# Chunked linear recurrence and squared-ReLU feed-forward: K, B, V and A turned by transposing DMAs, first feed-forwards one batch at a time

## The chip, the cores and the metric

The kernel runs on one core of a Trainium2 chip. The metric is the device time of one execution in microseconds (us); lower is better. The engines are called by the profile's names: PE is TensorE (PEld its weight loads), DVE VectorE, ACT ScalarE, POOL GpSimd and SP SyncE, which here only issues DMAs.

## The reference

Six inputs r, k, v, w, a, b have the shape (4, 8, 768, 40): batch, heads, time, head dimension. A state of 40 x 40 for each of 32 heads runs over time, and its output goes through a feed-forward with 2048 hidden units.

```python
for t in range(S):
    y[:, :, t] = np.einsum('bhd,bhde->bhe', rt, state)
    Sa = np.einsum('bhde,bhe->bhd', state, at)
    state_decay = state * wt[:, :, None, :] - np.einsum('bhd,bhe->bhde', Sa, bt)
    state = state_decay + np.einsum('bhd,bhe->bhde', vt, kt)
x = y.transpose(0, 2, 1, 3).reshape(B * S, H * D)      # 3072 x 320
g = np.maximum(x @ w_in, 0.0) ** 2                     # 3072 x 2048
out = g @ w_out                                        # 3072 x 320
```

Inputs and outputs are float32; the kernel multiplies in bfloat16, save for the cumulative sum of the logarithms of w, which is float32.

## The kernel before, in words

**Tiling.** Time is cut into six chunks of 128. The code calls a *batch* m one chunk of one batch element: m runs from 0 to 23, four to a chunk. A batch holds 128 positions (partitions) by 8 heads by 40. A *step* st is two of the four head pairs of a batch, so there are 48 steps. A pair of heads is padded to 2 x 64 = 128 columns, so that one 128 x 128 transpose on PE turns one pair.

**Preparation of a batch** (`add_prep`). SP loads six tiles of 160 KB (W, K, B, A, V, R; line 244), each in a ring of four buffers ("N"), so loads can run four batches ahead. ACT takes the logarithm of W (L257), PE the cumulative sum (cs, L263), ACT its exponentials GI and GA (L268). POOL multiplies K and B by GI into KB (L279; for the first two batches DVE takes B) and casts A into GA, and V and R into RV (L290), and V into EVX (L285). PE turns three sets, eight transposes each, all at line 294: tGA (GA and A), tKB (K and B) and tRV (R and V), each into one PSUM bank. The banks are emptied by ACT (GT, L330; KBT, L342) and DVE (AT = turned A times GT, L336; RVT, L347). KB has a ring of five buffers, GA and RV of two each, KBT of three.

**A step of the scan** (`add_step`). PE multiplies KBT by AT (ca, L394), DVE masks the product (CN, L402), PE forms P (L411, L417) and corrects it twice (L426) with ACT's Mc (L529) and DVE's c1 (L439) between them, ACT writes Sn (L536), POOL keeps two check values (x1, L443; Cc, L447). A later part turns back Sn (L463, L469; DVE TB, L474), multiplies by the turned R and V (ex, L482), masks (DVE EVX, L487), multiplies by KB (kbm, L498) and by the turned R (z, L505). DVE then writes the step's output YS (L511) and the state for the next chunk (UZ, L515).

**Feed-forward** (`add_ff`), for two batches together (h = 0 to 11). Four small DMAs of SP gather the last heads' rows of YS (mv, L628). Then come eight pieces, each of two blocks of 128 hidden units: PE with three matmuls of 256 columns for each block (hp, L638), ACT's ReLU (hs, L644), the square by POOL for three pieces of four and by DVE for the fourth (Gt, L649). Last come 16 matmuls for each batch with the second weight (op, L666), ACT's copy (L670) and SP's store (L675). POOL issues the loads of the weights WIN (L602) and WOUT (L609) in the first chunk.

**What sets the order.** Each piece of work is an `op` with an engine, a rank, a cost, a latency, its needs and its buffers. A list scheduler in the kernel, `listed`, plays the engines forward by these costs when the program is built: it takes at each point the op of lowest rank among those that can start. The order it finds is the fixed order of the instructions on each engine; no cost has another effect on the chip, where an engine waits for its next instruction. Buffers come from rings of the sizes in `RING`, and PSUM from eight banks, of which feed-forward holds at most four. On SP, every DMA also waits for the one eight before it. DMA time before the change is a latency of 2.9 for a load and a row of dummy ops on SP for the weights (`share`).

Of the kernel before, what the change touches and what calls it, by code (L numbers as in the profile page):

```python
# [18 lines left out]
def kernel(  # L19
# [42 lines left out]
            "AT": 3, "GT": 5, "CN": 3, "c1": 3, "x1": 3, "jk": 1, "jm": 1, "Mc": 2, "Cc": 2,  # L62
            "TB": 9, "UZ": 2, "YS": 3, "hs": 3, "Gt": 2, "osb": 3}
# [9 lines left out]
    class Op:  # L73
        __slots__ = ("name", "eng", "rank", "cost", "lat", "needs", "bufs", "mode", "fn", "end",
                     "order")
# [11 lines left out]
    def op(name, eng, rank, cost, lat, needs, bufs, fn, mode=None):  # L87
        o = Op()
        o.name, o.eng, o.rank, o.cost, o.lat, o.mode = name, eng, rank, cost, lat, mode
        o.needs, o.bufs, o.fn, o.end, o.order = list(needs), list(bufs), fn, None, len(ops)  # L90
        for b_ in o.bufs:
            b_.users.append(o)
        assert name not in ops, name
        ops[name] = o
# [24 lines left out]
    def pe(n):  # L119
        return n, n + 0.165  # L120

# [90 lines left out]
    SPLIT = 1  # L212

# [4 lines left out]
    for m in range(NBC):  # L218
# [7 lines left out]
        o.parts = [(0, 2), (2, 2)] if m < SPLIT else [(0, PB)]  # L226

# [10 lines left out]
    def add_load(m, key, rank):  # L238
        o = bt[m]
        c, bb = divmod(m, NB)  # L240

        def go():
            t_ = sb(o.nat[key], [128, NHH, D], FP32)
            nc.sync.dma_start(
                out=t_[:],
                in_=nat_srcs[key][bb, :, c * L:(c + 1) * L, :].rearrange("h t e -> t h e"))
        op(("L", m, key), "SP", rank, 0.97, 2.9, [], [o.nat[key]], go)

    def add_prep(m):
# [26 lines left out]
        def kb(u, key, j0, n):  # L276
            h = slice(2 * j0, 2 * j0 + 2 * n)
            eng = nc.vector if (m < 2 and key == "B") else nc.gpsimd
            eng.tensor_tensor(out=o.KB.tile[:, u, h, 0:D], in0=o.nat[key].tile[:, h],  # L279
                              in1=o.GI.tile[:, h], op=ALU.mult)  # L280

        def cast(key, j0, n):
            h = slice(2 * j0, 2 * j0 + 2 * n)
            if key == "X":
                nc.gpsimd.tensor_copy(  # L285
                    out=o.EVX.tile[:, j0:j0 + n, :, L:LV].rearrange("p i s e -> p (i s) e"),
                    in_=o.nat["V"].tile[:, h])
            else:
                pad = {"A": o.GA.tile[:, 1], "R": o.RV.tile[:, 0], "V": o.RV.tile[:, 1]}[key]
                nc.gpsimd.tensor_copy(out=pad[:, h, 0:D], in_=o.nat[key].tile[:, h])  # L290
# [5 lines left out]
        for p, (j0, n) in enumerate(o.parts):  # L296
# [6 lines left out]
            for u, key in enumerate("KB"):  # L303
                on = "DVE" if (m < 2 and key == "B") else "POOL"
                cost = 0.55 * f + 0.04 if on == "DVE" else 0.8 * f + 0.03
                op(("kb", m, key, p), on, sp - 2.2 + 0.1 * u, cost, cost + 0.07,
                   [("L", m, key), ("GI", m)] + cleared("KB", m), [o.nat[key], o.GI, o.KB],
                   lambda u=u, key=key, j0=j0, n=n: kb(u, key, j0, n))
            for x, (key, ring) in enumerate((("A", "GA"), ("V", "RV"), ("R", "RV"), ("X", "EVX"))):
# [4 lines left out]
                   lambda key=key, j0=j0, n=n: cast(key, j0, n))  # L314
            b1, b2, b3 = (buf("bank", "prep") for _ in range(3))

            def t_ga(b1=b1, j0=j0, n=n):
                turn(bank(b1), [o.GA.tile[:, u, 2 * j:2 * j + 2, :].rearrange("p a b -> p (a b)")
                                for u in range(2) for j in range(j0, j0 + n)])
# [5 lines left out]
            def t_rv(b3=b3, j0=j0, n=n):  # L325
                turn(bank(b3), [o.RV.tile[:, u, 2 * j:2 * j + 2, :].rearrange("p a b -> p (a b)")
                                for u in range(2) for j in range(j0, j0 + n)])

            def e_gt(b1=b1, j0=j0, n=n):
                nc.scalar.activation(  # L330
                    out=o.GT.tile[:, j0:j0 + n, 1:L + 1], func=ACTF.Copy,
                    in_=bank(b1)[:, 0:n * L].rearrange("p (j t) -> p j t", t=L))

            def e_at(b1=b1, j0=j0, n=n):
# [3 lines left out]
                    in0=bank(b1)[:, n * L:2 * n * L].rearrange("p (j t) -> p j t", t=L))  # L338

            def e_kb(b2=b2, j0=j0, n=n):  # L340
                t_ = sb(o.KBT, [128, 2, PB, L], BF16)
                nc.scalar.activation(  # L342
                    out=t_[:, :, j0:j0 + n], func=ACTF.Copy,
                    in_=bank(b2)[:, 0:2 * n * L].rearrange("p (u j t) -> p u j t", u=2, t=L))

            def e_rv(b3=b3, j0=j0, n=n):
                nc.vector.tensor_copy(  # L347
                    out=o.RVT.tile[:, :, j0:j0 + n, 0:L],
                    in_=bank(b3)[:, 0:2 * n * L].rearrange("p (u j t) -> p u j t", u=2, t=L))

            op(("tGA", m, p), "PE", sp - 1.9, *pe(0.45 * f), [("GA", m), ("cast", m, "A", p)],
               [o.GA, b1], t_ga, "F")
            op(("GT", m, p), "ACT", sp - 1.8, *act(512 * f), [("tGA", m, p)] + cleared("GT", m),
               [b1, o.GT], e_gt)
            op(("AT", m, p), "DVE", sp - 1.6, 0.075 + 0.267 * f, 0.16 + 0.267 * f, [("GT", m, p)],
               [b1, o.GT, o.AT], e_at)
            op(("tKB", m, p), "PE", sp - 1.3, *pe(0.45 * f), [("kb", m, key, p) for key in "KB"],
               [o.KB, b2], t_kb, "F")
            op(("KBT", m, p), "ACT", sp - 1.1, *act(1000 * f), [("tKB", m, p)], [b2, o.KBT], e_kb)
            op(("tRV", m, p), "PE", sp - 0.6, *pe(0.45 * f),  # L360
               [("cast", m, "V", p), ("cast", m, "R", p)], [o.RV, b3], t_rv, "F")
            op(("RVT", m, p), "DVE", sp - 0.4, 0.065 + 0.535 * f, 0.145 + 0.535 * f,
               [("tRV", m, p)] + cleared("RVT", m), [b3, o.RVT], e_rv)
# [12 lines left out]
    def add_step(st):  # L376
# [65 lines left out]
        def x1():  # L442
            nc.gpsimd.tensor_tensor(out=sb(x1b[st], [128, 4, D], FP32)[:], in0=M(),  # L443
                                    in1=c1b[st].tile[:], op=ALU.add)

        def cc():
            nc.gpsimd.tensor_tensor(out=C(), in0=x1b[st].tile[:], in1=Sn(), op=ALU.add)  # L447
# [24 lines left out]
        def tb_ev():  # L472
            hi = 4 if carry else 2
            nc.vector.tensor_copy(out=sb(TB_, [128, 4, 128], BF16)[:, 0:hi], in_=tbv()[:, 0:hi])  # L474

        def ex_mm():
            R, V = o.RVT.tile[:, 0], o.RVT.tile[:, 1]
            for u in range(2):
                for i in range(2):
                    for s in range(2):  # L480
                        lhsT = TB_.tile[half(s), i, :] if u else V[half(s), j0 + i, 0:L]
# [39 lines left out]
        for s in range(2):  # L521
# [7 lines left out]
           lambda: nc.scalar.activation(out=M(), func=ACTF.Copy, in_=Pv()))  # L529
# [6 lines left out]
           lambda: nc.scalar.activation(out=Sn(), in_=Pv(), func=ACTF.Copy, scale=-1.0))  # L536
        op(("jk", st), "ACT", st + 0.9, *act(512, 0.092), [("CN", st, 0), ("CN", st, 1)],
           [CN_, jkb[st]], jk)
        op(("x1", st), "POOL", st + 0.9, 0.43, 0.487, [("c1", st)], [Mcb[c], c1b[st], x1b[st]], x1)
        op(("Cc", st), "POOL", st + 1.0, 0.43, 0.487, [("x1", st), ("Sn", st)],  # L540
           [x1b[st], o.EVX, Ccb[c]], cc)
# [4 lines left out]
        op(("TB", st), "DVE", st + 2.2, 0.065 + 0.00052 * n, 0.146 + 0.00052 * n, [("tb", st)],  # L546
           [tbb, TB_], tb_ev)
# [43 lines left out]
    def share(name, issue, n, each):  # L591
        for i in range(n):
            last = i == n - 1
            op(name if last else (*name, i), "SP", -5.0, each, each + 2.0 * last,
               [(*name, i - 1) if i else issue], [], lambda: None)

    def add_weights():
        for g in range(NG):
# [6 lines left out]
            op(("WINi", g), "POOL", 0.5 + 0.5 * g, 0.52 * n, 0.52 * n, [("WIN2",), GATE[g]], [], go)  # L605
            share(("WIN", g), ("WINi", g), n, 0.7)
# [3 lines left out]
        op(("WOUTi",), "POOL", 2.5, 1.23, 1.3, [GATE[3]], [], go)  # L610
        share(("WOUT",), ("WOUTi",), 9, 0.92)
        op(("WIN2",), "DVE", -5.0, 1.0, 1.1, [], [], lambda: nc.vector.memset(WIN[2][:], 0.0))

    Gtb = [buf("Gt") for _ in range(NH)]

    def add_ff(h):
        c, hf = divmod(h, 2)
        st0 = c * NQ + hf * (NQ // 2)
        done = [("YS", st0 + i) for i in range(NQ // 2)]
        X_ = YSb[c]  # L620

        def by_pair():
            return X_.tile[:].rearrange("e (b p) t -> e p b t", b=NB)[:, :, HB * hf:HB * hf + HB, :]

        for x, (p, row, hh, e0, n) in enumerate(MOVED):
# [3 lines left out]
            op(("mv", h, x), "SP", st0 - 9.0 + 0.01 * x, 0.82, 2.0, done, [X_], gather)  # L629
        for jj in range(NJ // 2):  # L630
            hpb, hsb = buf("bank", "ff"), buf("hs")

            def ff_in(jj=jj, hpb=hpb):
                hp = hpb.tile[:].rearrange("p (u a b) -> p u a b", u=2, a=HB)
                for u in range(2):
                    j = 2 * jj + u
# [319 lines left out]
```

## Time and profile before

| | |
|---|---|
| median of 3 runs (lowest to highest) | 294.0 us (293.79 to 295.83) |
| the profiled execution, its own time | 294.21 us |
| its span, first to last instruction | 292.5 us |
| mean granted TensorE clock | 0.967 |
| busy PE, PEld, DVE, ACT, POOL | 272.7, 216.1, 227.7, 201.2, 202.9 us |
| DMA: the hardware queue (SP), the software queue (POOL) | 28.03 MB, 53.8% of 16 engines; 2.62 MB, 5.7% |

A row of the profile that names a line holds the engine, the operation, the tile written and the tiles read, the shapes, the count, the busy time and the mean of one in ns, then the idle time just before these instructions and what ended it. Records of matmuls that follow each other overlap, so the mean of one matmul is longer than its share of PE's time. SP's time is not counted as busy.

### The profile page before, as it was taken

Reading aid. Unit: us, or ns where it says so; the run is one execution under the profiler, and the core shown is the slowest. Engines: PE = TensorE matmul, PEld = TensorE weight load, DVE = VectorE, ACT = ScalarE, POOL = GpSimd, SP = SyncE. Lnnn points to the kernel's source line nnn. Section 1 sums busy time; section 2 is a strip of 40 time slices with the busy share of each in tenths; the row PEclk is TensorE's granted clock in tenths of the full one; section 3 lists DMA queues with packets and bytes.
Section 4 is the critical chain, followed back from the end, with each engine's and each line's share of the span. In section 5 each row is a group of like instructions: output and inputs, shape, how many; then the busy total and the mean of one; then the engine's idle time right before and its main releaser. Section 6 shows DMA issues by size and latency. Waiting matters only on the chain.

```text
span 292.5 us, 9938 instructions
## 1 busy us (share of the span) xinstructions
PE 272.7 (93%) x3852; PEld 216.1 (74%) x3852; DVE 227.7 (78%) x523; ACT 201.2 (69%) x531; POOL 202.9 (69%) x350
## 2 busy tenths in 40 slices
PE   6897879799998999999999999999999999999991
PEld 4665647487776788878788888888888888777871
DVE  7869988537699999999987987987987887771120
ACT  3657565387978689687687696796695776644641
POOL 7799654659998849887867878868868556555400
PEclk9959789799999999999999999999999999999998
DMA  7999794599999596978959958920010010001111
GB/s 135 180 175 183 122 174 80 102 175 180 170 173 165 101 175 120 163 136 139 192 98 178 172 101 152 145 53 25 2 31 22 2 31 25 10 23 33 44 48 53
DMA packets 158472, 31.37 MB, mean 107 GB/s; under 512 B 152976, under 2 KB 158096, under 8 KB 158416
## 3 DMA queue, kind: packets, MB, share of 16 engines
q1 hardware_dynamic: 155808, 28.03, 53.8%
q0 software_dynamic: 2608, 2.62, 5.7%
q8 instruction: 32, 0.52, 0.8%
q14 instruction: 24, 0.20, 0.2%
HBM read 28.84 MB, written 3.93 MB: 112 GB/s over the span
## 4 chain that ended last, share of the span: by engine, by line
PE 72%; DVE 9%; POOL 7%; ACT 6%; issue 2%; DMA 1%; POOLq 0%; DVEq 0%; ACTq 0%
PE bank L638 20%; PE bank L666 17%; PE bank L294 9%; PE bank L498 5%; PE bank L263 4%; PE bank L394 4%; PE bank L426 3%; PE bank L482 3%; DVE EVX L487 3%; DVE CN L402 3%; PE bank L505 2%; POOL KB L279 2%; PE bank L463 2%; ACT jk L451 2%; PE bank L469 1%
## 5 line engine op out<-in xcount | busy, mean ns | idle before, releaser
L649 POOL TENSOR_TENSOR Gt<-hs 128x512 bf16<-128x512 bf16 x66 | 68.6, 1043 | 23.0 <-ACT hs L644 22.0
L638 PE MATMUL bank<-YS,WIN 120*128 120x256 bf16 (+1 forms) x576 | 77.0, 273 | 0.0
L487 DVE TENSOR_TENSOR EVX<-bank,MEX 128x512 bf16<-128x512 f32 x96 | 64.9, 683 | 11.4 <-PE bank L482 9.2
L644 ACT ACTIVATE hs<-bank 128x512 bf16<-128x512 f32 x96 | 57.5, 601 | 22.5 <-PE bank L638 20.0
L402 DVE TENSOR_TENSOR CN<-bank,MCN 128x512 bf16<-128x512 f32 x96 | 64.5, 679 | 1.1 <-PE bank L394 1.1
L666 PE MATMUL bank<-WOUT,Gt 128*128 128x320 bf16 x384 | 60.2, 301 | 0.3 <-ACT GA L268 0.2
L638 PEld LDWEIGHTS <-WIN 120*128 120x128 bf16 (+1 forms) x576 | 51.8, 97 | 9.9 <-issue 0.6
L451 ACT ACTIVATE jk<-CN 128x512 bf16<-128x512 bf16 x48 | 30.3, 631 | 23.5 <-DVE CN L402 23.4
L666 PEld LDWEIGHTS <-Gt 128*128 128x128 bf16 x384 | 36.0, 98 | 13.5 <-issue 0.5
L443 POOL TENSOR_TENSOR x<-Mc,c 128x160 f32<-128x160 bf16 x48 | 23.5, 490 | 22.5 <-DVE c L439 21.9
L342 ACT ACTIVATE KBT<-bank 128x1024 bf16<-128x1024 bf16 (+1 forms) x25 | 24.7, 988 | 6.9 <-PE bank L294 6.8
L649 DVE TENSOR_TENSOR Gt<-hs 128x512 bf16<-128x512 bf16 x30 | 14.2, 473 | 19.6 <-ACT hs L644 19.3
L426 PEld LDWEIGHTS <-CN 128*128 128x128 bf16 x384 | 21.5, 98 | 10.3 <-issue 4.9
L279 POOL TENSOR_TENSOR KB<-NK,GI 128x320 bf16<-128x320 f32 (+1 forms) x25 | 21.2, 846 | 9.6 <-ACT GI L268 9.1
L447 POOL TENSOR_TENSOR Cc<-x,EVX 128x160 bf16<-128x160 f32 x48 | 23.7, 493 | 5.7 <-ACT EVX L536 4.9
L498 PE MATMUL bank<-EVX,KB 128*64 128x168 bf16 x384 | 23.7, 243 | 1.6 <-DVE EVX L487 1.6
L474 DVE COPY TB<-bank 128x512 bf16<-128x512 bf16 (+1 forms) x48 | 18.6, 393 | 3.7 <-PE bank L469 1.8
L511 DVE TENSOR_TENSOR YS<-bank,GT 128x256 bf16<-128x256 f32 x48 | 20.2, 420 | 1.1 <-PE bank L505 0.6
L439 DVE TENSOR_TENSOR c<-bank,Mc 128x160 bf16<-128x160 f32 x48 | 15.1, 317 | 7.3 <-PE bank L426 7.1
L394 PE MATMUL bank<-AT,KBT 64*128 64x128 bf16 x384 | 19.6, 226 | 1.2 <-DVE AT L336 1.1
L515 DVE TENSOR_TENSOR UZ<-bank,GT 64x80 bf16<-64x80 f32 x80 | 18.8, 235 | 1.9 <-PE bank L498 0.8
L263 PE MATMUL bank<-lnW,UTI 128*128 128x320 f32 x48 | 19.6, 491 | 0.8 <-DVE EVX L487 0.4
(82 smaller groups left out, 535.1 us busy)
## 6 DMA issues: line engine op xcount, KB each, us to landing
NW<-in_w_dram SPq DMA_DIRECT2D x24, 160.0 KB
NK<-in_k_dram SPq DMA_DIRECT2D x24, 160.0 KB
NB<-in_b_dram SPq DMA_DIRECT2D x24, 160.0 KB
NA<-in_a_dram SPq DMA_DIRECT2D x24, 160.0 KB
NV<-in_v_dram SPq DMA_DIRECT2D x24, 160.0 KB
NR<-in_r_dram SPq DMA_DIRECT2D x24, 160.0 KB
out_dram<-osb SPq DMA_DIRECT2D x24, 160.0 KB
WOUT<-in_moe_w_out_dram POOLq DMA_DIRECT2D x1, 1280.0 KB, 10.6
```

Of the source, the lines that this page charges most:

```text
L263: nc.tensor.matmul(out=csb.tile[:, 0:NHH * D], lhsT=UTI[:], rhs=o.lnW.tile[:], start=True, stop=True)
L279: eng.tensor_tensor(out=o.KB.tile[:, u, h, 0:D], in0=o.nat[key].tile[:, h], in1=o.GI.tile[:, h], op=ALU.mult)
L394: nc.tensor.matmul(out=quads(ca[s])[:, i, u, :], lhsT=o.KBT.tile[half(s), u, j0 + i, :], rhs=o.AT.tile[half(s), j0 + i, :], start=(i == 0 ...
L402: nc.vector.tensor_tensor(out=t_[:, :, s], in0=quads(ca[s]), in1=MCN[:], op=ALU.mult)
L426: nc.tensor.matmul(out=P[:, 2 * i + s], lhsT=CN[:, i, s, 1, :], rhs=X[:, 2 * i + s], start=False, stop=last, skip_group_check=True)
L451: nc.scalar.activation(out=t_[:], in_=CN_.tile[:, :, :, 1, :], func=ACTF.Square, accum_out=ACC[:, AN + st:AN + st + 1])
L487: nc.vector.tensor_tensor(out=EVX[:, :, s, 0:2 * LV].rearrange("p i (u x) -> p i u x", u=2)[:, :, :, 0:L], in0=quads(ex[s]), op=ALU.mult, ...
L498: nc.tensor.matmul(out=uy()[half(s), i, :], lhsT=o.KB.tile[:, u, 2 * (j0 + i) + s, :], rhs=EVX[:, i, s, LV * u:LV * u + LV], start=(i == 0 ...
L638: nc.tensor.matmul(out=hp[:, u], lhsT=WIN[g][0:ROWS[g], j * 128:(j + 1) * 128], rhs=by_pair()[0:ROWS[g], g], start=(g == 0 and u == 0), st ...
L644: nc.scalar.activation(out=sb(hsb, [128, 512], BF16)[:], in_=hpb.tile[:], func=ACTF.Relu)
L649: eng.tensor_tensor(out=t_[:, 2 * jj:2 * jj + 2].rearrange("p j a b -> p (j a b)"), in0=hsb.tile[:], in1=hsb.tile[:], op=ALU.mult)
L666: nc.tensor.matmul(out=opb.tile[:, 0:DM], lhsT=Gtb[h].tile[:, j, b_, :], rhs=WOUT[:, j, :], start=(j == 0), stop=(j == NJ - 1))
```

## The change

Three things change.

1. *Turning by DMA.* For batches m from 6 on, SP turns all of KB (128 x 1024, bfloat16) into KBT by one transposing DMA from SBUF to SBUF, in place of eight PE transposes, a bank and ACT's KBT. For batches from 12 on, one such DMA turns A (128 x 512) into a new tile A0, of two buffers, and one turns V into its half of RVT; tGA and tRV then have four PE transposes each, AT reads A0, and RVT's copy is half as long. c1 and x1 have two buffers instead of three.
2. *Feed-forward.* The first four batches go singly, the others in pairs as before. A single batch has four pieces, each of four blocks of 128 hidden units, with matmuls of 128 columns. There are 14 feed-forwards (56 gathering DMAs) instead of 12 (48).
3. *The scheduler's costs.* DMAs are played on two queues, "h" for SP's and "s" for POOL's, that delay each other. PE's costs are 1.4 times as high up to 56 us of the plan. Gathers and turns get some time of grace.

`op` also takes `alts`, other engines for the same work. `listed` does not read them: each op stays on the engine that it is given first, and the counts of DVE's, ACT's and POOL's instructions differ by the evictions named under 1 and by squares of 4 x 128 instead of 512.

```diff
-            "AT": 3, "GT": 5, "CN": 3, "c1": 3, "x1": 3, "jk": 1, "jm": 1, "Mc": 2, "Cc": 2,
-            "TB": 9, "UZ": 2, "YS": 3, "hs": 3, "Gt": 2, "osb": 3}
+            "AT": 3, "GT": 5, "CN": 3, "c1": 2, "x1": 2, "jk": 1, "jm": 1, "Mc": 2, "Cc": 2,
+            "A0": 2, "TB": 9, "UZ": 2, "YS": 3, "hs": 3, "Gt": 2, "osb": 3}
...
+    BY_DMA = {"KB": range(6, NBC), "V": range(12, NBC), "A": range(12, NBC)}
...
-        op(("L", m, key), "SP", rank, 0.97, 2.9, [], [o.nat[key]], go)
+        op(("L", m, key), "SP", rank, 0.78, 0.78, [], [o.nat[key]], go)
+        ops["L", m, key].dma = "h", 0.85
...
+            a_d, kb_d, v_d = (m in BY_DMA[x] for x in ("A", "KB", "V"))
+
+            def across(out, in_):
+                nc.sync.dma_start_transpose(out=out, in_=in_)
+
+            def d_a():
+                across(sb(o.A0, [128, PB, L], BF16)[:], o.GA.tile[:, 1].rearrange("p a b -> p (a b)"))
+
+            def d_kb():
+                across(sb(o.KBT, [128, 2, PB, L], BF16)[:].rearrange("p u j t -> p (u j) t"),
+                       o.KB.tile[:].rearrange("p u a b -> p (u a b)"))
+
+            def d_v():
+                across(o.RVT.tile[:, 1].rearrange("p j x -> p (j x)")[:, 0:PB * L]
+                       .rearrange("p (j t) -> p j t", t=L),
+                       o.RV.tile[:, 1].rearrange("p a b -> p (a b)"))
...
+            def turning(name, rank, needs, bufs, fn):
+                op((name, m, p), "SP", rank, 0.8, 0.8, needs, bufs, fn)
+                ops[name, m, p].dma = "h", 0.8 if name != "KBT" else 1.6
...
+            if a_d:
+                turning("A0", sp - 5.0, [("cast", m, "A", p)], [o.GA, o.A0], d_a)
+            op(("AT", m, p), "DVE", sp - 1.6, 0.075 + 0.267 * f, 0.16 + 0.267 * f,
+               [("GT", m, p)] + [("A0", m, p)] * a_d, [o.A0 if a_d else b1, o.GT, o.AT], e_at)
+            if kb_d:
+                turning("KBT", sp - 5.0, [("kb", m, key, p) for key in "KB"], [o.KB, o.KBT], d_kb)
+            else:
+                op(("tKB", m, p), "PE", sp - 1.3, *pe(0.45 * f), [("kb", m, key, p) for key in "KB"],
+                   [o.KB, b2, o.KBT], t_kb, "F")
...
+            if v_d:
+                turning("VT", sp - 4.0, [("cast", m, "V", p)], [o.RV, o.RVT], d_v)
+            op(("tRV", m, p), "PE", sp - 0.6, *pe(rv * f),
+               [("cast", m, "R", p), ("cast", m, "V", p)][:2 - v_d] + [("VT", m, p)] * v_d,
+               [o.RV, b3, o.RVT], t_rv, "F")
...
+    FFS = [(0,), (1,), (2,), (3,)] + [(m, m + 1) for m in range(4, NBC, 2)]
...
+        ms = FFS[h]
+        c, b0 = divmod(ms[0], NB)
+        nb, last = len(ms), 2 * ms[-1] + 1
+        NU = 4 // nb
...
-            rank = st0 + 12.0 + 0.45 * jj
+            rank = last + 9.0 + 0.225 * NU * jj
...
-    LATE = {"mv": 2.5, "st": 6.0}
+    LATE = {"mv": 2.5, "st": 6.0, "A0": 1.5, "KBT": 1.5, "VT": 1.5}
     BIAS = {"FR": 0.3, "FC": 0.6, "CR": 0.3}
+    COLD = 56.0, 1.4
...
+            slow = COLD[1] if e == "PE" and t < COLD[0] else 1.0
+            free[e] = t + o.cost * slow
+            o.end = t + o.lat + o.cost * (slow - 1.0)
+            if o.dma:
+                kind, work = o.dma
+                begin = max(dq[kind], t + 0.4)
+                if kind == "h":
+                    over = max(0.0, dq["s"] - begin)
+                    shared = min(work, over / 2)
+                    dq["s"] += shared
+                    dq["h"] = begin + work + shared
+                    free[e] = max(free[e], dq["h"] - 2.0)
+                else:
+                    dq["s"] = begin + work + min(work, max(0.0, dq["h"] - begin))
+                o.end = max(o.end, dq[kind]) + 1.6
```

More of the change, by code (lines that the diff above doesn't have):

```diff
@@ new lines, in add_prep @@
+            if v_d:
[3 more added lines that the diff above has]
+               [o.RV, b3, o.RVT], t_rv, "F")
+            n_ = 512 if v_d else 1024
+            op(("RVT", m, p), "DVE", sp - 0.4, *vec(n_ * f, 0.00052),
+               [("tRV", m, p)] + cleared("RVT", m), [b3, o.RVT], e_rv, alts=[("ACT", *act(n_ * f))])
@@ L652, in add_ff, with relu @@
-            rank = st0 + 12.0 + 0.45 * jj
-            on = "POOL" if jj % 4 and h < NH - 1 else "DVE"
-            op(("hp", h, jj), "PE", rank, *pe(0.654),
+            def relu(eng, hpb=hpb, hsb=hsb):
+                t_ = sb(hsb, [128, 512], BF16)[:]
+                if eng == "ACT":
+                    nc.scalar.activation(out=t_, in_=hpb.tile[:], func=ACTF.Relu)
+                else:
+                    nc.vector.tensor_scalar(out=t_, in0=hpb.tile[:], scalar1=0.0, scalar2=None,
+                                            op0=ALU.max)
@@ L661, in add_ff @@
-        for b_ in range(HB):
+            op(("hs", h, jj), "ACT", rank + 0.3, *act(500), [("hp", h, jj)], [hpb, hsb], relu,
+               alts=[("DVE", *vec(512))])
+            op(("Gt", h, jj), ways[0][0], rank + 0.6, *ways[0][1:], [("hs", h, jj)], [hsb, Gtb[h]],
+               square, alts=ways[1:])
+        for b_ in range(nb):
             opb, osbb = buf("bank", "ff"), buf("osb")
```

213 lines of the change are left out of this document (115 added, 98 removed).

## The prediction

> **What bounds the kernel now.** I read the page's slices first, then the busy time in stretches of 10 us, then the chain that ended last, then TensorE's own timeline.
>
> ```profile
> span 292.5 us, 9938 instructions
> PE 272.7 (93%) x3852; PEld 216.1 (74%) x3852; DVE 227.7 (78%) x523; ACT 201.2 (69%) x531; POOL 202.9 (69%) x350
> PE   6897879799998999999999999999999999999991
> DMA  7999794599999596978959958920010010001111
> PE 72%; DVE 9%; POOL 7%; ACT 6%; issue 2%; DMA 1%; POOLq 0%; DVEq 0%; ACTq 0%
> ```
>
> PE is at nine tenths from the ninth slice (about 60 us) to the last; 72% of the chain is PE. The DMA row is as full up to slice 26 (190 us) and nearly empty behind it.
>
> ```profile
> 50.00:60.00 10.00, 7.96 (x82) 5.94 (x80) 4.43 (x8) 4.39 (x9) 6.26 (x10) 0.83 0.58 101
> 60.00:70.00 10.00, 10.00 (x144) 7.99 (x143) 6.47 (x14) 8.36 (x27) 7.50 (x13) 1.00 1.00 178
> 120.00:130.00 10.00, 9.99 (x172) 8.00 (x168) 9.70 (x25) 6.90 (x19) 9.01 (x17) 1.00 0.92 155
> 200.00:210.00 10.00, 9.97 (x156) 8.12 (x154) 8.10 (x19) 7.58 (x20) 7.82 (x13) 1.00 0.05 18
> ```
>
> The columns are PE, PEld, DVE, ACT, POOL, the granted clock, the DMA share and GB/s. There are three regimes: a start with gaps on PE and a reduced clock; 90 to 150 us, where PE and DVE are both full (DVE 9.1 to 9.9); and from 150 us on PE alone (9.94 to 10.00 up to 280), with DVE at 6.7 to 9.0 up to 260. So what leaves PE after 60 us shortens the run, as long as nothing else takes its place.
>
> ```profile
> 204.61 0.62 PE L294 MATMUL bank<-IDb,KB 128*128 128x128 bf16 x8
> 205.07 0.31 PE L505 MATMUL bank<-RVT,TB 128*128 128x168 bf16 x2
> ...
> 264.08 0.42 DVE L511 TENSOR_TENSOR YS<-bank,GT 128x256 bf16<-128x256 f32 x1 [0.58 <-PE bank L505]
> ...
> 282.05 4.51 PE L666 MATMUL bank<-WOUT,Gt 128*128 128x320 bf16 x32
> ```
>
> From the start of eight transposes to the start of what follows are 0.46 us; three other groups near by give 0.44, 0.44 and 0.45. So a transpose costs the PE stream 0.056 us, not the 0.232 us of its own record, since matmuls overlap. The scan ends with the last YS at 264.1; behind it stands feed-forward that PE works off without a gap.
>
> **The change part by part.** *Transposes off PE.* K and B of 18 batches are 18 x 8, A and V of 12 batches are 12 x 4 each: 240 of 576 transposes go. 240 x 0.056 = **13.5 us less on PE**, all of it after 60 us. The instruction list of the changed program bears out the count, and leaves the same 22 us of PE work behind the last YS as before, so the saving must show as an earlier end of the scan.
>
> *Evictions.*
>
> ```profile
> L342 ACT ACTIVATE KBT<-bank 128x1024 bf16<-128x1024 bf16 (+1 forms) x25 | 24.7, 988 | 6.9 <-PE bank L294 6.8
> L347 DVE COPY RVT<-bank 128x1024 bf16<-128x1024 bf16 (+1 forms) x25 | 16.5, 662 | 2.8 <-PE bank L294 2.7
> ```
>
> ACT loses 18 KBT evictions of 1.02 us (the full form), 18 us; it was idle for 31% of the span, so this counts as nothing. DVE's RVT halves 12 times; its smaller form took 0.41 where the full one took 0.68, so 3.2 us go. AT reads A0 from SBUF, at the 0.41 us it costs now or less. POOL's work does not change.
>
> *Is DVE then the bound?* From 150 to 260 us it was busy for 92.4 of 110 (84%). If the scan ends 13.5 us sooner, 89.2 stand in 96.5 (92%). Between 90 and 140 us, with DVE at 97 to 98%, PE still was 98.8% busy, against 99.8% later. One point of some 110 us: **plus 1.1 us**.
>
> *Feed-forward of the first four batches singly.* Sixteen pieces of 12 matmuls of 128 columns replace 16 of 6 with 256. By the transpose's 0.056 a piece is 0.67 us, against 0.66: plus 0.2 us. Eight more moves (YS to YS) go to SyncE, 0.82 us each, early, where it has room. At the start the pieces can fill gaps (PE idles 4.9 us between 30 and 60) or bring another 3.4 us window of half clock (1.7 us lost): between -4.9 and +1.7. I take 0, because from 30 to 60 us PE waits on DVE and POOL, which keep their work.
>
> *The turning DMAs.* SyncE issues 18 of 256 KB and 24 of 128 KB. No row shows one. By bytes at the loads' rate (160 KB in 0.92 us at 178 GB/s, 60 to 70 us) they take the queue 1.47 and 0.74 us. As the low end, by packets of 256 B at the loads' rate of 1024 packets in 0.92 us: 0.92 and 0.46. As the high end, by WOUT, which landed 1280 KB in 10.6 us beside loads: 2.12 and 1.06. I take the middle, since such a turn shares the loads' queue and is nearest to them in size: 18 x 1.47 + 24 x 0.74 = 44.2 us (27.6 to 63.6). Less than nothing they can't take, as the queue loses no transfer.
>
> What hides them: between 60 and 190 us the DMA shares sum to 113.9 us, so 16 are free; the last KBT eviction was at 236.7, so the last turn is wanted about 223, and from 190 to 223 another 30 are free. That is 46 us, and the program places a K/B turn some 12 us of PE work ahead of its first use (7 to 8 for the first two, 11 to 17 later), so **58 us are covered: nothing is added**, with 14 to spare. If the cover goes, each further us shows in full, first as PE waiting in its order for KBT (L394), behind which the feed-forward pieces stand too; at the high end 5.6 us do.
>
> The Trainium skill ("DMA: Bandwidth & Descriptors", section "Latency and other measured facts") gives 261 GB/s for a DMA transpose with a non-contiguous middle dimension. By it (an estimate) the turns take 1.0 and 0.5 us, 30 in all, and the sum stays; no run here shows it.
>
> *New waits.* A turn waits on SyncE for POOL's product or cast; behind it stand loads (needed two batches later), stores and moves. GA and RV, two buffers each, are freed by the turns: POOL's next cast of A comes 10 us of PE work or more after the turn's issue, of V 6 or more; TensorE's RV transposes now wait for V's turn and DVE's AT for A's, both issued 6 us or more ahead. c1 and x1 have two buffers instead of three: DVE's c then waits for POOL's x of two steps earlier, some 10 us back. I cost these at nothing; without cover the first to stand is POOL, and PE behind KB.
>
> *The sum.* 292.5 - 13.5 + 0.2 + 1.1 = 280.3 us of span; with the 1.7 us between this profile's span and its run (294.2), **282.0 us**. That run was 0.2 above the median of 294.0, which does not move the figure.
>
> **The rivals.** *One: the DMA queue becomes the bound, and it is slower.* The place is SyncE's queue from the seventh batch on. It starts to cost above 58 us of turns (1.93 us for 256 KB) and decides against the change at 58 + 12.2 = 70 us (2.3 us). For it speaks the DMA row: at 0.97 or more in seven of the thirteen ten-us stretches from 60 to 190, so it is near its limit there. Against it: the two unlike kinds of transfer that the trace has, loads and WOUT, would leave the turns covered or cost 5.6 us. At twice the byte price, 88.4 us: 282.0 + 30.4 = 312 us.
>
> *Two: every 128x128 block is a transfer of its own.* At the 0.82 us that SyncE takes to issue a small move, a K/B turn takes 6.6 us and the others 3.3: 197 us, of which 139 show, 421 us. Nothing in the profile speaks for it but that no turn was seen. The Trainium skill ("VectorE: DVE Perf Modes", section "The three transpose paths") speaks for it: 1309 ns for a block by DMA against 390 on TensorE. By that (an estimate) the turns would take 314 us; the trace has TensorE's block at 56 ns in the stream, so its figures are for a block alone.
>
> *Three: DVE sets the pace up to 150 us.* Then what leaves PE before that brings nothing: K and B of nine batches and A and V of three, 96 transposes, 5.4 us: 287 us. For it: DVE 9.7 to 9.9 between 90 and 140. Against it: PE was as full there, and feed-forward done earlier is feed-forward spared later.
>
> *Four: the gain is eaten by waits of the new order, near 294.* For it: the turns tie POOL, SyncE and PE more closely together. Against it: the leads above. That the change does not do what it says can be left out, as the instruction list has 42 turns and 240 transposes fewer.
>
> **How the numbers follow.** Forecast 0.58 (own range 276 to 289: the start's -4.9 with no loss to DVE, or its +1.7 with the dear end of the turns, +5.6), three 0.14, four 0.05, one 0.20, two 0.03. Within 1% is about what a measurement of this kernel cannot tell from no change. Faster by over 1%: 0.58 + 0.14 = 0.72; within 1%: 0.05; slower: 0.23. The range runs from 276 to 303: below it lies little, and above it the dearer half of one, and two.
>
> **What would show it.** Right: 336 transposes in the L294 kind of group; PE still above 99% from 150 us; the last YS near 252 us and about 22 us of feed-forward behind it; DMA near 1.00 up to some 215 us; turns that take 1.5 us of queue for 256 KB; no wait of PE for KBT. Wrong: PE or its weight loads waiting for KBT, A0 or V's turn, loads that land after 225 us, DVE above 97% past 150 us while PE idles, or a start that reaches the sixth batch's cumulative sum (L263 at 60.7 us now) some us earlier or later.

## The result, and the profile after

The changed kernel takes 315.3 us (median of 4 runs, 313.86 to 317.1), the kernel before beside it 294.9: a ratio of 1.069 (1.061 to 1.077). It is slower by 20 us where 12 us less were forecast. The profiled execution took 313.86 us with a span of 312.1 and a mean granted clock of 0.927 (0.967 before).

The page of the changed kernel: span, busy time, two rows of the slices, SyncE's queue (packets, MB, share of 16 engines) and the chain that ended last.

```profile
span 312.1 us, 9670 instructions
PE 271.8 (87%) x3708; PEld 212.2 (68%) x3708; DVE 226.1 (72%) x523; ACT 185.9 (60%) x513; POOL 205.6 (66%) x350
PE   6888959899998799789499887699799899999992
DMA  7999987697996999587796997997997940000111
q1 hardware_dynamic: 187984, 35.90, 70.9%
PE 42%; DMA 22%; SPq 13%; DVE 9%; POOL 5%; issue 4%; ACT 4%; POOLq 0%; DVEq 0%; ACTq 0%
```

PE was 72% of the chain and is 42; DMA and SP's queue, 1% together before, are 35. The DMA row stays full for a further 60 us or so, and PE's row, nine tenths nearly throughout from 60 us before, has holes up to slice 32 (250 us).

The same columns as the stretches before (PE, PEld, DVE, ACT, POOL, granted clock, DMA share, GB/s), the first four in stretches of ten us, the last of 30:

```profile
50.00:60.00 10.00, 9.25 (x156) 7.02 (x156) 9.88 (x25) 7.37 (x20) 5.69 (x10) 0.93 0.65 111
60.00:70.00 10.00, 9.04 (x160) 7.76 (x158) 8.59 (x21) 7.31 (x24) 8.17 (x16) 1.00 0.80 137
120.00:130.00 10.00, 7.76 (x109) 5.82 (x109) 8.69 (x19) 6.21 (x20) 9.69 (x17) 1.00 1.00 118
200.00:210.00 10.00, 9.04 (x88) 6.31 (x88) 7.57 (x18) 4.18 (x14) 7.77 (x13) 0.66 1.04 173
180.00:210.00 30.00, 24.20 (x311) 18.20 (x309) 19.34 (x45) 15.48 (x46) 18.64 (x30) 0.89 0.95 150
```

Summed from 90 to 240 us in such stretches, PE stands idle for 20.3 us, against 0.8 before. The granted clock fell as well: 0.89, 1.00, 0.89, 0.89, 0.94 in the five stretches, 1.00 in all five before, which is at most (0.11 x 3 + 0.06) x 30 = 11.7 us. Idle time and clock together make 31.2, the transposes give 13.5 by the forecast's price, and the 17.7 that are left come near the 19.6 by which the span grew. So nearly all of the loss lies between 90 and 240 us.

What the engines wait for of DMAs, some rows of the table of waits (engine, tile and line that waited, what for: total us, times, longest):

```profile
ACT lnW L282 <- DMA NW<-in_w_dram: 23.4, 11, 5.3
POOL GA L230 <- DMA NA<-in_a_dram: 15.4, 12, 3.0
DVE AT L379 <- DMA A<-GA: 14.2, 6, 4.1
POOL RV L230 <- DMA RVT<-RV: 4.8, 4, 2.4
POOL KB L303 <- DMA NB<-in_b_dram: 3.5, 1, 3.5
```

The first line was 1.7 us in one wait before, the second 3.2 in two. The logarithm of W is the first step of a batch's preparation, and the load of W was late ten times (the other wait is for the kernel's first load, as before). PE itself has no wait for KBT. The timelines of SP, ACT and PE show one such case:

```profile
93.51 3.15 SPq L346 DMA_TRANSPOSE KBT<-KB  x1
96.75 3.22 SPq L689 DMA_DIRECT2D YS<-YS  x4
100.02 0.58 SPq L268 DMA_DIRECT2D NW<-in_w_dram  x1
...
103.05 0.47 ACT L282 ACTIVATE lnW<-NW 128x320 f32<-128x320 f32 x1 [2.58 <-DMA NW<-in_w_dram]
103.58 1.44 PE L288 MATMUL bank<-lnW,UTI 128*128 128x320 f32 x2 [2.16 <-ACT lnW L282]
```

A turn of K and B and four moves hold SP for 6.5 us; only then is W's load issued, at 100.02, and 3.0 us later ACT takes its logarithm at once. Before, for the batches m = 12 to 23, this lead from the issue to the logarithm was 5.8 to 27.1 us; it is now 3.0 to 5.8. PE stood for 2.16 us, and its two matmuls took 1.44 behind it. The kernel's first load, with no other DMA of SP ahead of it, shows what a load needs:

```profile
0.83 0.46 SPq L268 DMA_DIRECT2D NW<-in_w_dram  x1
3.73 0.47 ACT L282 ACTIVATE lnW<-NW 128x320 f32<-128x320 f32 x1 [1.63 <-DMA NW<-in_w_dram]
```

That is 2.9 us; nine of the ten late ones took 3.0 to 3.3, one 4.7. So a late load came about as fast as the very first: it was issued late.

SP's own instructions in the trace of the changed kernel (count, then shortest, median and longest in ns, first and last start):

```profile
L346 SPq DMA_TRANSPOSE KBT<-KB x18: 1231/1344/3145, 71.2 to 251.0; - x18
L346 SPq DMA_TRANSPOSE A<-GA x12: 1190/1211/2362, 121.3 to 247.1; - x12
L346 SPq DMA_TRANSPOSE RVT<-RV x12: 1188/1320/2555, 133.1 to 249.0; - x12
L268 SPq DMA_DIRECT2D NW<-in_w_dram x24: 462/577/1946, 0.8 to 229.9; - x24
L689 SPq DMA_DIRECT2D YS<-YS x56: 533/764/2076, 42.5 to 287.6; - x56
```

The page does not count this time as busy, but SP is occupied for it: it issues one DMA after the other. A turn holds it for 1.2 us at least, whether it turns eight blocks (KBT) or four, and 1.56 on average (65.6 us for 42). Summed over its timeline, SP issued for 54.4, 50.7 and 17.5 us of the 60-us stretches from 60, 120 and 180 us before the change, and for 55.6, 55.7 and 55.8 after it. It had little room before 180 us. Not all of this time is need: the same 144 loads held SP for 126.8 us before, for 122.9 here and for only 105.9 in the run with small idle turns below, where the queue is emptier.

### The profile page after: what moved, and what is told of

It is laid out like the page before. It is cut to its first block, busy times and chain, and to the rows that moved or that the text cites. A ratio compares the mean times of both kernels' runs of the same rounds, so it can differ in the third digit from the quotient of the medians.

```text
span 312.1 us, 9670 instructions
## 1 busy us (share of the span) xinstructions
PE 271.8 (87%) x3708; PEld 212.2 (68%) x3708; DVE 226.1 (72%) x523; ACT 185.9 (60%) x513; POOL 205.6 (66%) x350
## 3 DMA queue, kind: packets, MB, share of 16 engines
q1 hardware_dynamic: 187984, 35.90, 70.9%
## 4 chain that ended last, share of the span: by engine, by line
PE 42%; DMA 22%; SPq 13%; DVE 9%; POOL 5%; issue 4%; ACT 4%; POOLq 0%; DVEq 0%; ACTq 0%
PE bank L700 13%; PE bank L737 12%; SPq L268 8%; DMA NV<-in_v_dram 7%; DMA NW<-in_w_dram 5%; DMA A<-GA 4%; DMA NB<-in_b_dram 4%; SPq L689 4%; PE bank L561 3%; DVE EVX L550 3%; DVE CN L461 3%; DMA NA<-in_a_dram 2%; PE bank L318 2%; PE bank L288 2%; PE bank L453 2%
## 5 line engine op out<-in xcount | busy, mean ns | idle before, releaser
L700 PE MATMUL bank<-YS,WIN 120*128 120x256 bf16 (+3 forms) x672 | 80.2, 262 | 5.0 <-DVE EVX L550 2.9
L700 PEld LDWEIGHTS <-WIN 120*128 120x128 bf16 (+1 forms) x672 | 56.3, 99 | 16.2 <-issue 5.4
L737 PE MATMUL bank<-WOUT,Gt 128*128 128x320 bf16 x384 | 61.8, 306 | 0.9 <-DVE TB L230 0.9
L561 PE MATMUL bank<-EVX,KB 128*64 128x168 bf16 x384 | 25.6, 257 | 0.5 <-DVE EVX L550 0.5
L282 ACT ACTIVATE lnW<-NW 128x320 f32<-128x320 f32 x24 | 11.2, 468 | 23.6 <-DMA NW<-in_w_dram 23.4
L227 ACT ACTIVATE EVX<-bank 128x160 bf16<-128x160 f32 x48 | 14.4, 299 | 18.0 <-PE bank L485 15.5
L288 PE MATMUL bank<-lnW,UTI 128*128 128x320 f32 x48 | 21.3, 530 | 3.6 <-ACT lnW L282 3.2
L230 POOL CAST GA<-NA 128x320 bf16<-128x320 f32 (+1 forms) x25 | 11.1, 443 | 16.4 <-DMA NA<-in_a_dram 15.4
L303 POOL TENSOR_TENSOR KB<-NB,GI 128x320 bf16<-128x320 f32 x22 | 19.2, 873 | 3.5 <-DMA NB<-in_b_dram 3.5
L453 PE MATMUL bank<-AT,KBT 64*128 64x128 bf16 x384 | 21.0, 233 | 0.6 <-DVE AT L379 0.6
```

The source lines that it names most:

```text
L288: nc.tensor.matmul(out=csb.tile[:, 0:NHH * D], lhsT=UTI[:], rhs=o.lnW.tile[:], start=True, stop=True)
L303: engine(eng).tensor_tensor(out=o.KB.tile[:, u, h, 0:D], in0=o.nat[key].tile[:, h], in1=o.GI.tile[:, h], op=ALU.mult)
L453: nc.tensor.matmul(out=quads(ca[s])[:, i, u, :], lhsT=o.KBT.tile[half(s), u, j0 + i, :], rhs=o.AT.tile[half(s), j0 + i, :], start=(i == 0 ...
L561: nc.tensor.matmul(out=uy()[half(s), i, :], lhsT=o.KB.tile[:, u, 2 * (j0 + i) + s, :], rhs=EVX[:, i, s, LV * u:LV * u + LV], start=(i == 0 ...
L700: nc.tensor.matmul(out=hp[:, u], lhsT=WIN[g][0:ROWS[g], j * 128:(j + 1) * 128], rhs=by_pair()[0:ROWS[g], g], start=(g == 0 and u == 0), st ...
L737: nc.tensor.matmul(out=opb.tile[:, 0:DM], lhsT=Gtb[h].tile[:, j, b_, :], rhs=WOUT[:, j, :], start=(j == 0), stop=(j == NJ - 1))
```

## The experiments

In the expectations, theory S is that SyncE's own time to issue is what ran out; theory T that it is the transfers on the hardware queue; theory P, from the replanned run on, that the scheduler's wrong costs for the turns made the loss. All ratios are to the kernel before.

**No turns.** The rest of the change stays.

```diff
-    BY_DMA = {"KB": range(6, NBC), "V": range(12, NBC), "A": range(12, NBC)}
+    BY_DMA = {"KB": range(0), "V": range(0), "A": range(0)}
```

> The changed kernel with every turn back on TensorE; the single feed-forwards and the scheduler's new costs stay. Theory T (the turns cost the DMA engines 2.13 us for 256 KB, 63.9 us in all by the queue's share before and after, and the loads come late): without turns the loads have their lead again and TensorE has 13.5 us more work than in the changed kernel, so about 294 us, within 3 of the kernel before. Theory S (SyncE's issue in order is the bound, turns hold it 1.2 to 3.1 us each): the same, about 294. Theory F (the single feed-forwards or the new costs of the scheduler spoil the order): stays over 305.

298.3 us, 1.015 (1.007 to 1.023). The turns make 17 of the 20 us, and the rest of the change 3.4, which the interval makes uncertain by 2.3. In its stretches PE's gaps against before are in 30 to 60 (22.5 busy of 30, before 25.1) and 90 to 120 us (27.8, before 29.6), and from 120 to 240 PE is as full as before.

**K and B alone.** `"V": range(0), "A": range(0)`.

> Only K and B are turned by DMA, V and A by TensorE again. Theory T: 24 turns at 1.06 us leave the queue, 25.5 us; TensorE has 5.4 us more. The changed kernel lies 33 us above the forecast 282, so 31 of the 64 us of turns are covered; 38 us of turns leave 7 uncovered: 282 + 5.4 + 7 = 294. Theory S: 24 issues of at least 1.2 us leave SyncE, 29 us and the waits for POOL with them, nearly the whole excess: about 288. Theory F: over 305.

299.5 us, 1.0145 (1.010 to 1.019): 18 turns cost 1 us net, which the intervals don't tell from nothing; the other 24 cost 16. The queue's busy time, its share times the span, is 65.8% x 298.3 = 196.3 us against 54.1% x 295.7 = 160.0 without turns: 2.0 us for a turn of 256 KB. From here to the changed kernel (70.9% x 312.1 = 221.3) 24 turns of 128 KB add 25 us, 1.04 each.

**Moves and stores issued by ScalarE.**

```diff
-                nc.sync.dma_start(out=by_pair()[row:row + n, p], in_=by_pair()[src:src + n, hh // 2])
+                nc.scalar.dma_start(out=by_pair()[row:row + n, p], in_=by_pair()[src:src + n, hh // 2])
...
-                nc.sync.dma_start(out=out[tok:tok + L, :], in_=osbb.tile[:])
+                nc.scalar.dma_start(out=out[tok:tok + L, :], in_=osbb.tile[:])
```

> The changed kernel with its stores and its gathering moves issued by ScalarE instead of SyncE, in the same places of the order: 80 DMAs fewer on SyncE, 56 x 0.76 + 24 x 0.52 = 55 us of its issue time; the bytes are the same. Theory S: loads get their lead back, 285 to 295. Theory T: the DMA engines have the same work, so 312 to 318; ScalarE has the time to spare (60% busy).

328.0 us, 1.111 (1.103 to 1.120): no theory's number. Two of its waits:

```profile
ACT KBT L227 <- DMA YS<-YS: 18.1, 1, 18.1
ACT lnW L282 <- DMA NW<-in_w_dram: 2.4, 2, 1.6
```

With SP relieved, W came in time (2.4 us of waits instead of 23.4), but ACT, which works in order, now stood for 18.1 us at once behind two of its own DMAs, of which the first began only at 55.15 us, 16 us after ACT's work before it. How much of the loss this wait and others like it make was not worked out. The run does not tell the theories apart; the two were told apart later, without another engine.

**Turns only from batch 20 on**, where the slices of before show an empty queue: all three `range(20, NBC)`.

> Turns for the last four batches alone (K, B, A and V), when the loads are nearly over. Theory T: 4 x 4.25 = 17 us of turns fall where the queue was nearly empty in the kernel before, so TensorE keeps 4 x 16 x 0.056 = 3.6 us: 3 to 4 us below the kernel without turns, about 290. Theory S: the same sign, about 290 to 293, as each turn still holds SyncE's queue ahead of stores and moves. Theory F: over 305.

296.4 us, 1.005 (1.001 to 1.008): 12 turns that take 64 transposes off PE bring 1.9 us against no turns, within the noise of the two; by 0.056 it would be 3.6. The queue's time is 57.4% x 296.3 = 170.1, 10 us above no turns, 1.26 us by 256 KB, with the DMA share at 0.35 to 0.39 from 180 to 240 us: much less than beside the loads.

**Turns of one block each.** All 42 turns stay, each of 128 x 128 alone; the rest of KBT, A0 and V's turn is left as it was (of A0 and V's part, POOL first sets it to zero), so the products are of other data.

```diff
-                across(sb(o.KBT, [128, 2, PB, L], BF16)[:].rearrange("p u j t -> p (u j) t"),
-                       o.KB.tile[:].rearrange("p u a b -> p (u a b)"))
+                across(sb(o.KBT, [128, 2, PB, L], BF16)[:].rearrange("p u j t -> p (u j) t")[:, 0:1],
+                       o.KB.tile[:].rearrange("p u a b -> p (u a b)")[:, 0:L])
```

> The changed kernel, in its own order, but every turn moves only one 128x128 block (of eight in K and B, of four in V and A); what it leaves out of KBT, A0 and V's half of RVT stays as earlier batches wrote it or zero, so the result is not the reference's. SyncE still issues 42 turns and waits for the same work of POOL. Theory T (the bytes of the turns keep the DMA engines from the loads): some 11 us of turns instead of 64, all covered: the forecast 282 plus the 3.5 us that the kernel without turns lies above the kernel before, 285. Theory S (issue of at least 1.2 us each and the waits in SyncE's order): as the changed kernel, 310 to 315.

The whole took 14932.9 us, since these data make the kernel run its general branch after the main part; only the main part can be read. Its last osb on ACT, and then the same of the changed kernel (the line is the kernel's own):

```profile
297.31 0.44 ACT L229 ACTIVATE osb<-bank 128x320 f32<-128x320 f32 x1 [0.65 <-PE bank L747]
```
```profile
305.97 0.44 ACT L227 ACTIVATE osb<-bank 128x320 f32<-128x320 f32 x1 [0.65 <-PE bank L737]
```

Leaving out most of the turned bytes brings 8.7 us, which lies between what S (310 to 315) and T (285) expect. In the kernel before the last osb stood at 286.6. The DMA share was only 0.57 to 0.69 in the 30-us stretches from 120 to 240, and yet 10.7 us are lost.

**Idle turns, large and small.** The kernel without turns gets 54 turns of constant data (WOUT) into a scratch tile that nobody reads, ahead of the loads of W, B and V of batches from 6 on: of three blocks in the first run, of one in the second. Nothing waits for their data, and the scheduler does not know of them.

```diff
+            if key in "WBV" and m >= 6:
+                flat = WOUT[:].rearrange("p j f -> p (j f)")
+                nc.sync.dma_start_transpose(out=SCR["WBV".index(key)][:, 0:3], in_=flat[:, 0:3 * L])
```

> The kernel without turns, in its own order, with 54 idle turns added in SyncE's queue, three for each batch from the seventh on, ahead of the loads of W, B and V: each turns three blocks of a weight into a tile that nobody reads. TensorE does all transposes, nothing waits for a turn, and a turn waits for nothing but the queue. Theory T: 54 x 0.78 = 42 us more of the queue, 31 of them covered: 298 + 11 = 309. Theory S: 54 x 1.2 = 65 us more of issue time: 315 or more. Theory W (the waits between turns, POOL and TensorE, and not the queue, are what costs): 298 to 301.

> As the kernel with 54 idle turns, but each turns one block instead of three. Theory T: 54 x 0.26 = 14 us of the queue, covered: 298 to 300. Theory S: the same as with three blocks, 315 or more, as the issue time hardly depends on the size (1.19 us at least for 128 KB, 1.23 for 256 KB). Theory W: 298 to 300.

335.9 us, 1.141 (1.135 to 1.147), with three blocks; 334.5 us, 1.1355 (1.1285 to 1.1425), with one. SP's turns and its queue, first of the large, then of the small:

```profile
L270 SPq DMA_TRANSPOSE SCR<-WOUT x54: 1177/1318/2305, 52.6 to 233.7; - x54
q1 hardware_dynamic: 178384, 33.35, 59.1%
```
```profile
L270 SPq DMA_TRANSPOSE SCR<-WOUT x54: 1095/1272/2455, 52.5 to 234.1; - x54
q1 hardware_dynamic: 164560, 29.81, 49.8%
ACT lnW L287 <- DMA NW<-in_w_dram: 21.9, 7, 6.5
```

A third of the bytes, the same time: both lose 36 to 38 us against no turns, with the DMA share at 0.59 to 0.75 from 60 to 240 us in the second, and W late as in the changed kernel. SP's time for the turns is nearly the same in both, 75.2 and 72.8 us. This speaks for S, and against T; the loss is larger than either expected. An unplanned microsecond of SP costs about half a microsecond of the run here.

**Feed-forward in pairs throughout**, without turns: `FFS = [(m, m + 1) for m in range(0, NBC, 2)]`.

> The kernel without turns, with all feed-forwards in pairs as in the kernel before; the scheduler's new costs and the two buffers of c1 and x1 stay. If the single feed-forwards cost the 3.5 us: 294 to 295.5. If the new costs or the buffers do: 297 to 299.

Three of its four runs took 302.6 to 304.1 us, the fourth 297.8, as with single feed-forwards (298.3). With this spread the run decides nothing: the singles are not shown to cost anything.

**No moves, after and before.** The gathering moves of SP are left out, so that the last heads' rows of the feed-forward hold padding; the order of everything else stays.

```diff
-                src = 64 * (hh % 2) + e0
-                nc.sync.dma_start(out=by_pair()[row:row + n, p], in_=by_pair()[src:src + n, hh // 2])
+                pass
```

> The changed kernel in its own order without the 56 gathering moves of YS on SyncE (so the last two heads' rows of the feed-forward hold padding, and the result is not the reference's). The moves are 48 us of SyncE's issue time and only 0.5 MB. Theory S (SyncE's queue, issued one after the other, is full, and the 42 turns put 66 us into it): some 30 us of the 48 lie between the first turn and the last load, so the loads get about that back: 285 to 293. Theory T (bytes on the DMA engines): 308 to 315, less at most the 4 us that feed-forward waited for moves.

> The control: the kernel before without its 48 moves (the result is not the reference's). It has no turns and its loads come in time, so both theories expect 292 to 295; a fall of more than 4 us would mean that the moves themselves, not SyncE's time, are what the run without moves gains.

The changed kernel falls by 24.5 to 290.8 us, 0.984 (0.978 to 0.991), the kernel before stays at 294.5, 0.9975 (0.994 to 1.001). With the same turns, and 0.49 MB less of the queue's 35.90, the queue is as full as ever; a stretch of the changed kernel, then the same stretch and W's wait without moves:

```profile
150.00:180.00 30.00, 26.40 (x367) 20.15 (x367) 24.95 (x60) 17.62 (x50) 21.76 (x35) 0.89 0.87 145
```
```profile
150.00:180.00 30.00, 29.84 (x458) 23.55 (x454) 28.00 (x66) 22.51 (x66) 25.75 (x41) 1.00 1.00 162
```
```profile
ACT lnW L282 <- DMA NW<-in_w_dram: 7.6, 5, 2.0
```

PE is busy for 29.84 of 30 us (26.40 with the moves) at a DMA share of 1.00: a full queue does not by itself stop PE. Nor does a full SP by itself: in this stretch SP issues for 27.7 of the 30 us, and for 27.6 in the changed kernel. What the moves' time bought is the lead: for m = 6 to 18, W is issued 6.2 to 14.4 us ahead of its logarithm, and 3.0 to 6.1 in the changed kernel. Still, the whole change brings only 3.7 us here against the kernel before without its moves, where 12 were forecast. What takes the rest was not tried apart; from 90 to 150 us DVE is busy for 58.95 of 60 us and PE for 57.0, and behind 180 us W's leads fall to 2.7 to 4.5.

**The plan with measured costs.** Same turns, but the scheduler counts what was measured: 1.56 us of SP for a turn, 2.02 and 1.04 us of queue, 0.92 for a load.

```diff
-        ops["L", m, key].dma = "h", 0.85
+        ops["L", m, key].dma = "h", 0.92
...
-                op((name, m, p), "SP", rank, 0.8, 0.8, needs, bufs, fn)
-                ops[name, m, p].dma = "h", 0.8 if name != "KBT" else 1.6
+                op((name, m, p), "SP", rank, 1.56, 1.56, needs, bufs, fn)
+                ops[name, m, p].dma = "h", 1.04 if name != "KBT" else 2.02
```

> The changed kernel planned with what its profile shows: a turn holds SyncE 1.56 us (planned 0.8) and the DMA engines 2.02 or 1.04 us (planned 1.6, 0.8), a load 0.92 (0.85). Theory P (the change costs time because the fixed order was made with too small costs, so that engines wait in the wrong places): 288 to 298. Theory S: SyncE has the same work to do before the last batch can start, so an order can't win it back: 303 to 313.

297.4 us, 1.011 (1.003 to 1.020). P is right for 18 us: the same work on a full SP (55.5, 55.3 and 55.7 of each 60 us) in a better order. S as first put, by which no order would help, falls. But the leads are still about 3 us, W is waited for 11.8 us, and the 240 transposes have brought no more than 1 us against no turns.

**The two costs one by one**: the SP cost alone, then the queue's alone.

> The changed kernel with one number of the plan changed: a turn holds SyncE 1.56 us instead of 0.8. If the turn's time on SyncE is the cost that the plan lacked: about as the plan with all measured costs, 296 to 302. If it was the time of bytes on the DMA queue: near the changed kernel, 308 to 316.

> The changed kernel with the plan's times on the DMA queue alone as measured: turns 2.02 and 1.04 us, loads 0.92; SyncE's 0.8 for a turn stays. If SyncE's time is what the plan lacked: 305 to 316. If the queue's time was: 296 to 302. As the plan holds SyncE back when its queue is over 2 us deep, dear bytes stand in for dear issues in part, so a result between is possible and would tell little.

303.8 us, 1.0325 (1.027 to 1.038), and 303.4, 1.027 (1.021 to 1.033). Each alone brings 12 of the 18 us, so they overlap, and which of them was the worse can't be said.

**Measured costs and no moves** (both edits above).

> The kernel planned with all measured costs, in its order, without its gathering moves (the last two heads' rows of the feed-forward hold padding). Theory S: SyncE is still full there (56, 55 and 58 us of each 60 between 60 and 240), so the loads get a lead again: 284 to 291. If what is left is something else (the order, POOL, DVE): 295 to 298.

292.05 us, 0.988 (0.983 to 0.993): 5.4 less than with the moves, 1.3 more than without moves under the old costs. From m = 6 on the leads are 8.6 to 12.8 us, and W is waited for once (1.7 us, the kernel's first load), but PE still has only 27.8 to 28.6 of each 30 us from 180 to 270. That plan has lateness of its own, and what makes it was not found.

**Fewer turns, and late.** The kernel before, with turns of K, B, A and V for the last five batches only, planned at 1.3 us of SP and 4.3 to landing, and none of the other parts (A0 and x1 have two buffers). Then also K and B from batch 14.

```diff
+    BY_DMA = range(19, NBC)
...
+            def turning(name, rank, needs, bufs, fn):
+                op((name, m, p), "SP", rank, 1.3, 4.3, needs, bufs, fn)
```
```diff
-    BY_DMA = range(19, NBC)
+    BY_DMA, KB_DMA = range(19, NBC), range(14, NBC)
```

> The kernel before, with its own scheduler's costs and pairs of feed-forwards, and turns by DMA for K, B, A and V of the last five batches alone (planned at 1.3 us of SyncE and 4.3 us to landing). Most of these turns come when SyncE has few loads left to issue, so theory S expects TensorE's 5 x 16 x 0.056 = 4.5 us back: 290 to 291. Theory T the same. If it is above 294, turns cost something that neither theory has.

> The kernel before with turns of A and V for the last five batches and of K and B for the last ten. Five more K/B turns take 40 transposes, 2.2 us, from TensorE and put 5 x 1.25 = 6 us into SyncE's queue between some 130 and 190 us, where the kernel with five late batches issued for 49 of 60 us. Theory S: it still fits, 287.5 to 290.5; if the loads lose their lead there, 292 or more.

290.5 us, 0.987 (0.981 to 0.992), and 289.4 us, 0.979 (0.974 to 0.983): both beat both kernels, the second not clearly the first. 80 and 120 transposes less at 0.056 us are 4.5 and 6.7 us; 4.4 and 5.5 were measured. The second in a stretch with turns:

```profile
180.00:210.00 30.00, 29.84 (x449) 23.88 (x448) 27.60 (x66) 21.27 (x62) 25.96 (x42) 1.00 0.88 147
```

PE is as full as before the change, at more than twice the DMA share (0.41 then). SP issues for 27.5 of these 30 us, and for 27.9 in the changed kernel (over the three stretches of 60 us for 52.9, 50.1 and 46.9), but W is waited for only once (1.6 us, the kernel's first load). So it is not SP's share as such that costs, but that the loads no longer get ahead.

## Why the prediction was wrong

The step that failed is "What hides them": "58 us are covered: nothing is added". The cover was the free share of the DMA engines, 46 us, with 12 of lead, and the turns were priced by bytes and packets alone. SP, which has to issue them, was left out of the sum (its time for an issue stands only in rival two), though the trace of before has its instructions: 105 of the 120 us from 60 to 180. Into that came 42 turns of 1.56 us, 65.6 us. They push the loads back until each lands as it is wanted; the chain is load of W, logarithm, cumulative sum, PE. There was little to push: loads behind a turn were taken as "needed two batches later", but in the trace of before W was issued only 4.7 to 9.1 us ahead of its logarithm for m = 6 to 17, about one batch. The same slip is in "Eight more moves ... early, where it has room": from 60 us on there was little. That SP's time decides is shown from both sides: time given back to it without touching the queue's load brings 24.5 us (no moves), time taken from it with few bytes costs 36 (idle small turns).

What turned a shortage into 20 us is the order. The scheduler counted 0.8 us of SP for a turn and 1.6 and 0.8 of queue, and so put turns and moves ahead of loads that were already late. With measured costs 18 us come back. The forecast's own price of the queue, 1.47 and 0.74, was near the plan's; neither had the 1.56 us of SP.

*The size of a turn.* I took 1.47 and 0.74 us of queue. Beside loads it was 2.0 and 1.04, the high end (2.12 and 1.06, from WOUT), for which the forecast allowed 5.6 us. The Trainium skill ("DMA: Bandwidth & Descriptors", section "Latency and other measured facts") gives 261 GB/s, by which 256 KB take 1.0 us; the nearest here is the 1.26 us of the late turns, with the queue at 0.35 to 0.39, and beside the loads it is twice the page's. The bytes do count for something: the one-block turns put their share at 8.7 us, though these also shorten the wait for a turn to land.

*Rival one* (312 us, 0.20) has the time and the engines of the chain, but not the cause. It put the bound in the transfers above 58 us of turns; measured they took 64 (221.3 less 157.4, before's 53.8% of 292.5), for which its rule gives 6 us. The queue at 1.00 did not stop PE in the run without moves. *Rival two* does not hold: a turn is one issue, at 1.2 us for eight blocks as for one. *Rival three* does not show in the changed kernel, where DVE is busy for 72% and waits; without the moves, when the loads have their lead again, DVE is busy for 98% from 90 to 150 us, and PE for 95%. *Rival four* is there as a part: DVE waits 14.2 us for A's turn, "issued 6 us or more ahead" and costed at nothing, and POOL 4.8 for V's. PE does not wait for KBT, as forecast.

*Right, as far as the runs go,* was the price of a transpose on PE (4.4 us measured for 80, 5.5 for 120, where the loads keep their lead; no run shows the 13.5 for all 240). *Right* was also the piece behind the scan. The last YS, which was to end near 252, and the last matmuls:

```profile
283.46 0.42 DVE L574 TENSOR_TENSOR YS<-bank,GT 128x256 bf16<-128x256 f32 x1 [0.49 <-PE bank L568]
...
301.42 4.51 PE L737 MATMUL bank<-WOUT,Gt 128*128 128x320 bf16 x32
```

From 283.5 to 305.9 are 22.4 us, as before (264.1 to 286.6): all that was lost was lost in the scan.

*The start and the single feed-forwards*, taken at 0 and 0.2, belong to the 3.4 us that the change costs without turns, nearly all before 120 us. The run in pairs does not show them coming back; the scheduler's new costs and the smaller rings of c1 and x1 were not tried apart, so this stays open.

In the sum: 282.0 us + 3.9 (the rest of the change: 294.2 + 0.2 forecast, 298.3 measured) + 29.4 (the turns: 12.4 less forecast, 17.0 more measured) = 315.3.

## What to carry to other kernels

Before work is moved to DMAs, add up the durations of the issuing queue's own instructions in the stretch where they go: an SP that issues for 50 to 55 of 60 us has hardly any room, whatever the share of the DMA engines says, and how far the loads are issued ahead of their use tells what it can still lose. A transposing DMA pays as long as the loads behind it keep their lead; here a third to a half of the turns, the late ones, brought 4 to 6 us, and all 42 lost 17. If a planner makes the order, its cost for a new kind of DMA has to be measured first: the same work took 297 or 315 us.

## What the runs showed of the hardware

The issue of a transposing DMA on SP lasted 1.1 us at the least for one block of 128 x 128 and 1.23 for eight (1095 and 1231 ns), where a load of 160 KB took 0.37 at its shortest and 0.85 on average; the size came back mainly in the queue's share. In the queue, the same turn cost 1.26 us by 256 KB late, at a DMA share of 0.35 to 0.39, and 2.0 beside loads of 160-byte rows. And two DMAs issued from ACT held up ACT's own work, in order, for 18.1 us at once.
